# A fused attention and gated feed-forward kernel: a new order for everything up to the middle of block 2

## The chip, the core and the metric

The kernel runs on one core of one Trainium2 chip. The metric is device microseconds of one execution. The kernel before takes 634.76 us (median of three runs, 634.62 to 634.83).

## What is computed

Attention over q, k, v of 4 batches, 8 heads, 768 positions, 64 columns: each query sees the 31 keys around it (|i - j| < 16) and 24 summaries, one for each block of 32 keys (the maximum of the keys, the mean of the values, log 32 added to the score). The result, as 3072 tokens of 512 columns, goes through a gated feed-forward:

```
scores_s = scale * q @ k_sum.T + log(32)         # k_sum: max, v_sum: mean of 32 rows
a = softmax(concat(where(|i-j| < 16, scale * q @ k.T, -1e9), scores_s))
x = a @ concat(v, v_sum)                         # 3072 x 512
h = x @ w_in;  g = h * cos(h);  out = g @ w_out  # 512 -> 2048 -> 512
```

All of it is in float32. For the feed-forward each operand is split into a high part and a rest (the low part), both of a faster float format, and three products (high-high, low-high, high-low) stand for one.

## The kernel before

**Tiling.** The 3072 tokens are 8 blocks of 384, two blocks for each batch. In a block the attention works on four groups a, b, c, d of two heads each (class Group, line 429). The feed-forward works in 128 steps (class Step, line 714): one step is one block and one of 16 slices of 128 hidden columns. Steps s0 to s5 are block 0 with slices 0 to 5, s6 to s21 block 1 with all 16, s22 to s31 block 0 with slices 6 to 15, and from s32 on come blocks 2 to 7.

**The order is written out by hand.** There is no scheduler: ORDER is a list of 2098 tokens, and the last lines of the kernel call one method for each in turn. An engine executes its instructions in the order of the tokens; waits follow from the data, from the buffers and from the eight PSUM banks that the tokens name. Where several engines can do a thing, the token's last letter says which: a is ScalarE, v is VectorE, p is GpSimd.

```
    with tc.manual_schedule(engines=everything):
        prepare()
        for token in ORDER.split():
            who, what, *args = token.split(".")
            one = whose[who]
            getattr(one, does[type(one)][what])(*(int(a) if a.isdigit() else eng_of[a] for a in args))
```

**Tokens of a group**, for instance a0 (group a, block 0):
- q, k, v load (two DMAs each for q and k in the first blocks, three for v, all on the SyncE queue, lines 454, 475, 483); k is loaded once for a batch.
- tk and tq turn k (by halves) and q on TensorE (lines 516, 503); ck and cq place them in SBUF; ks takes the maxima of the keys' blocks on VectorE (line 535).
- ms puts the masks into two PSUM banks by two products (line 554), sc adds the scores (48 products, line 579), mx takes the maxima on VectorE (two reductions, line 597), ex the exponentials with their sums on ScalarE (six, line 614), iv the inverse of the sums on VectorE (lines 624, 627), nm multiplies by it on GpSimd (line 630).
- tp turns the result on TensorE in two parts (line 639), cp places the parts, m copies the means of v beside v (24 rows), va does the values (24 products, line 683), xh and xl make the high and low part of x for the feed-forward (lines 370 or 372, and 376).
- From block 2 on other ways are taken for some of this (kt, qt, kw, z, su, sm, pt, po, pi).

**Tokens of a weight slice**, w0 to w15 (class Slice, line 382): l loads it (two DMAs, lines 391 and 395, 1.02 MB), ab takes one byte of each value apart and sh makes its first bits (ScalarE, lines 403 and 409), fb joins these bits with the rest (VectorE, line 416, two SBUF inputs), hi is the high part (a copy), lo the rest (line 376).

**Tokens of a step**: up is the projection (12 products, line 726), or u one chunk of it, that needs one group of x alone (3 products, line 738); tu, re, si, ga make h * cos(h) on ScalarE (746), VectorE (749), ScalarE (754), VectorE (758); hi and lo are the high and low parts of the result; dh and dl are six and three down products, with sums that stay in three PSUM banks over a run of steps (line 786); ta and st take and store the sums.

**Other tokens.** h0 to h7 are two products each whose result nobody reads (class Warm, line 927). v0_0 and v0_1 are the means of v in batch 0, done by products on TensorE (vm, line 909; ve places them). v1_0 to v1_7 are the means of batch 1: l loads (line 246), s sums (VectorE: lines 261, 270; GpSimd: lines 251, 267, 270). They are wanted by m of block 2.

## Time and profile before

| | |
|---|---|
| median of three runs | 634.76 us |
| the profiled execution, its own time | 633.6 us |
| its span, first to last instruction | 631.9 us |
| chain that ended last | PE 92%, DVE 4%, SPq 2% of the span |
| HBM read and written | 54.43 MB and 16.52 MB |
| first product of the feed-forward | starts at 41.23 us |
| first down product | starts at 58.30 us |

PE is the matmul side of TensorE and PEld its weight load, DVE VectorE, ACT ScalarE, POOL GpSimd, SP SyncE; a name with a q is the engine's queue. A time is in microseconds from the start of the span. A matmul's end is modelled, so that a busy PE need not be at its peak.

### The profile page before, as it was taken

How to read it: one execution, taken by the hardware profiler on the slowest of the kernel's cores; microseconds unless marked ns; L12 is line 12 of the kernel's file. 1: busy time of each engine (PE TensorE's matmuls, PEld its weight loads, DVE VectorE, ACT ScalarE, POOL GpSimd, SP SyncE). 2: the span in 40 equal slices, each digit the busy share in tenths (PEclk: the TensorE clock that was granted, in tenths of full speed). 3: DMA queues.
4: the chain of work that ended last, by engine and by line, in shares of the span. 5: the costliest groups of instructions: out<-in, count | busy, mean ns of one | idle time of the engine just before them, and what ended most of it. 6: DMA issues, size and time to landing. Idle time of an engine off the chain costs nothing.

```text
span 631.9 us, 12130 instructions
## 1 busy us (share of the span) xinstructions
PE 621.1 (98%) x4568; PEld 544.3 (86%) x4568; DVE 422.1 (67%) x814; ACT 323.9 (51%) x606; POOL 204.6 (32%) x218
## 2 busy tenths in 40 slices
...
GB/s 223 261 220 272 297 123 250 145 54 123 122 143 133 112 95 174 102 61 108 109 110 126 117 93 102 121 47 77 108 98 61 117 75 56 114 35 17 1 1 50
DMA packets 170058, 73.52 MB, mean 116 GB/s; under 512 B 136848, under 2 KB 158864, under 8 KB 170000
## 3 DMA queue, kind: packets, MB, share of 16 engines
...
HBM read 54.43 MB, written 16.52 MB: 112 GB/s over the span
## 4 chain that ended last, share of the span: by engine, by line
PE 92%; DVE 4%; SPq 2%; DMA 1%; issue 1%; ACT 1%; POOL 0%; POOLq 0%; DVEq 0%
PE banks L786 41%; PE banks L726 40%; PE banks L683 3%; PE banks L567 3%; PE banks L930 1%; SPq L475 1%; DVE stage L416 1%; PE banks L738 1%; PE banks L579 1%; SPq L483 1%; PE banks L516 0%; PE banks L909 0%; DMA late<-in_v_dram 0%; DMA x<-in_v_dram 0%; DVE kd L535 0%
## 5 line engine op out<-in xcount | busy, mean ns | idle before, releaser
L726 PE MATMUL banks<-xh,w 128*128 128x384 f32 x976 | 255.5, 337 | 0.5 <-DVE t L758 0.5
L786 PE MATMUL banks<-w,gh 128*128 128x512 f32 x768 | 196.5, 392 | 0.1
L726 PEld LDWEIGHTS banks<-xh,w 128*128 128x128 f32 x976 | 176.8, 188 | 3.1 <-issue 0.8
L786 PEld LDWEIGHTS banks<-w,gh 128*128 128x128 f32 x768 | 142.6, 188 | 31.4 <-DVE gh L372 1.8
L726 PE MATMUL banks<-xl,w 128*128 128x384 f32 x488 | 163.2, 334 | 0.0
L376 POOL TENSOR_TENSOR gl<-t,gh 128x384 fp32r<-128x384 f32 x63 | 65.9, 1048 | 283.3 <-DVE gh L372 147.8
L746 ACT ACTIVATE t<-banks 128x384 int32<-128x384 f32 x128 | 62.0, 488 | 126.8 <-PE banks L726 59.7
L749 DVE SCALAR_TENSOR_TENSOR t<-t,banks 128x384 f32<-128x384 int32 x128 | 69.1, 546 | 68.3 <-ACT t L746 67.6
L786 PE MATMUL banks<-w,gl 128*128 128x512 f32 x384 | 108.0, 392 | 0.0
L754 ACT ACTIVATE t<-t 128x384 f32<-128x384 f32 x128 | 65.9, 523 | 63.4 <-DVE t L749 63.1
L726 PEld LDWEIGHTS banks<-xl,w 128*128 128x128 f32 x488 | 91.6, 188 | 0.4
L758 DVE TENSOR_TENSOR t<-t,banks 128x384 f32<-128x384 f32 x128 | 69.4, 547 | 33.1 <-ACT t L754 32.1
L786 PEld LDWEIGHTS banks<-w,gl 128*128 128x128 f32 x384 | 71.6, 188 | 15.7 <-POOL gl L376 0.5
L370 ACT CAST gh<-t 128x384 fp32r<-128x384 f32 x66 | 33.5, 511 | 43.5 <-DVE t L758 25.5
L630 POOL TENSOR_TENSOR sc<-sc,r 128x720 f32<-128x720 f32 x28 | 39.0, 1392 | 43.5 <-DVE r L627 41.0
L602 POOL TENSOR_TENSOR sc<-sc,m 128x720 f32<-128x720 f32 x24 | 34.3, 1433 | 49.6 <-DVE m L594 49.6
L376 DVE TENSOR_TENSOR gl<-t,gh 128x384 fp32r<-128x384 f32 x65 | 36.8, 569 | 12.5 <-ACT gh L370 7.5
L372 DVE CAST gh<-t 128x384 fp32r<-128x384 f32 x62 | 23.1, 373 | 18.1 <-PE banks L786 14.9
L586 DVE SCALAR_TENSOR_TENSOR sc<-banks,mask 128x360 f32<-128x360 f32 x48 | 24.5, 523 | 12.5 <-PE banks L567 12.2
L620 DVE TENSOR_REDUCE r<-sc 128x6 f32<-128x726 f32 x24 | 21.6, 902 | 13.8 <-ACT sc L609 13.8
L376 POOL TENSOR_TENSOR w<-stage,w 128x1024 fp32r<-128x1024 f32 x8 | 19.8, 2470 | 31.3 <-DVE w L372 20.0
L609 ACT ACTIVATE sc<-sc 128x720 f32<-128x720 f32 x24 | 19.4, 807 | 19.0 <-POOL sc L602 18.8
...
## 6 DMA issues: line engine op xcount, KB each, us to landing
...
```

Of the source, the lines that this page charges most:

```text
L370: eng.copy(out=out, in_=in_)
L372: eng.tensor_copy(out=out, in_=in_)
L376: eng.tensor_tensor(out=lo, in0=src, in1=hi.bitcast(F32), op=ALU.subtract)
L586: nc.vector.scalar_tensor_tensor(out=self.sc.rearrange("p (c h) n -> p c h n", h=2)[:, :, hh, :], in0=self.sp[hh], scalar=SCALE, in1=mask[ ...
L602: nc.gpsimd.tensor_tensor(out=self.sc, in0=self.sc, in1=self.m.unsqueeze(2).broadcast_to([P, U, NK]), op=ALU.subtract)
L630: nc.gpsimd.tensor_tensor(out=self.sc, in0=self.sc, in1=self.r.unsqueeze(2).broadcast_to([P, U, NK]), op=ALU.mult)
L726: nc.tensor.matmul(out=self.h, lhsT=w_of(name, self.f)[:, c * P : (c + 1) * P], rhs=x_of(self.blk, part, c), start=n == 0, stop=n == last,)
L746: nc.scalar.activation(out=self.t.bitcast(I32), in_=self.h, func=AF.Copy, scale=1.0 / TWO_PI, bias=0.25)
L749: nc.vector.scalar_tensor_tensor(out=self.t, in0=self.t.bitcast(I32), scalar=-TWO_PI, in1=self.h, op0=ALU.mult, op1=ALU.add)
L754: nc.scalar.activation(out=self.t, in_=self.t, func=AF.Sin, scale=-1.0, bias=-0.5 * math.pi)
L758: nc.vector.tensor_tensor(out=self.t, in0=self.t, in1=self.h, op=ALU.mult)
L786: nc.tensor.matmul(out=accs[self.run][i], lhsT=g[:, i * P : (i + 1) * P], rhs=w_of(name, self.f), start=self.first and n == 0, stop=self.l ...
```

## The change

Only ORDER changes. The last 1539 of its 2098 tokens, from s20.ga (in the middle of block 2's attention), are the same in the same order. The first 559 are the same set of operations in a new order; the PSUM banks and buffers that they name are new in many, and 67 of them name another engine:

| operation | to VectorE | to ScalarE | to GpSimd |
|---|---|---|---|
| low parts (lo) | 7 from GpSimd | | 13 from VectorE |
| high parts (hi) | 10 from ScalarE | 11 from VectorE | |
| placing p, k, q (cp, ck, cq) | 6, 4, 2 from ScalarE | 2, 0, 3 from VectorE | |
| high part of x (xh) | 1 from ScalarE | 3 from VectorE | |
| means (m), windows (kw) | | 2 from GpSimd, 1 from VectorE | |
| sums of v1 (s) | | | 2 from VectorE |

The loads move too: w1 and w0 go ahead of most of q, k and v, and v1_0, which stood after v0_1, goes behind w4. The diff up to s20.ga (the rest only breaks the lines elsewhere):

```diff
--- before.py
+++ after.py
@@ -25,59 +25,59 @@
 ORDER = """
-h0.w.3 h2.w.0 h4.w.1 a0.k a0.q b0.q a0.tk.1.5 c0.k a0.tk.0.0 a0.ms.7.6 a0.ks.1 d0.k b0.tq.3 a0.ks.0 b0.k a0.tq.4 c0.q
-a0.ck.1.a a0.ck.0.a h7.w.5 b0.cq.a a0.cq.v a0.sc c0.tk.0.0 c0.tk.1.2 b0.tk.0.4 c0.ks.0 c0.ck.0.a a0.mx.0 w1.l.6 h5.w.1
-a1.q c0.tq.0 h1.w.1 d0.q a0.ex.0 c0.ck.1.v b0.ck.0.a d0.tk.0.6 c0.ks.1 a0.iv b0.tk.1.1 b0.ks.0 d0.tk.1.2 c0.ms.3.7
-c0.cq.v b0.ms.5.0 c0.sc v0_0.l d0.ck.1.a d0.ks.1 b0.ck.1.a d0.ks.0 b0.ks.1 d0.ck.0.v b0.sc w1.ab.0 b1.q w1.sh c0.mx.1
-h6.w.2 a1.tq.6 a1.ms.1.4 v0_1.l v1_0.l d0.tq.2 a1.cq.v c0.ex.1 d0.cq.a a1.sc d0.ms.6.2 d0.sc b0.mx.2 c1.q w1.fb a0.nm
-w1.hi.v a0.tp.1.3 b0.ex.2 v0_0.vm.0 d0.mx.0 d0.ex.3 v0_1.vm a0.v a0.cp.1.a w1.lo.p c0.iv a1.mx.1 v0_1.ve.a b0.iv
-b1.tq.5 a0.tp.0.3 b1.cq.v b1.ms.2.6 b1.sc w0.l.7 d0.iv c0.nm b0.nm a0.m.p d0.m.p b0.m.p d1.q v1_0.s.0.v a1.ex.0 h3.w.5
-a0.cp.0.v d1.m.p b1.mx.2 c0.m.p c1.tq.3 v1_1.l c0.tp.0.5 d0.nm c0.v a1.iv a1.nm a1.m.p c0.tp.1.0 a0.va.4 c1.ms.7.1 c1.cq.v
-c0.cp.0.v d1.tq.3 d0.v a0.xh.a c1.sc v1_1.s.p w2.l.6 b0.v d1.cq.v a0.xl w0.ab.1 b0.tp.1.3 b0.tp.0.5 c0.cp.1.v w0.sh
-d0.tp.0.4 c0.va.0 b1.ex.1 d0.tp.1.6 v1_2.l c1.mx.0 w5.l.1 w0.fb w0.hi.v a1.v w0.lo.p d0.cp.0.a c1.ex.2 b1.iv d0.cp.1.v
-c1.m.p d1.ms.4.2 c0.xh.v d1.sc c0.xl d0.va.0 b1.nm d1.mx.1 b0.cp.0.a b0.cp.1.v a1.tp.0.7 w2.ab.1 c1.iv a1.tp.1.6 c1.nm
-s1.u.0.3 w2.sh d0.xh.v d1.ex.3 d0.xl b0.va.1 b0.xh.v s0.u.0.5 b0.xl v1_2.s.p s0.u.2 s1.u.2 s1.u.3 a1.cp.0.v c1.tp.1.7
-s1.u.1 s0.u.3 w2.fb w2.hi.v a1.cp.1.a d1.iv d1.v c1.v c1.tp.0.2 s0.u.1 s1.tu.0 w4.l.6 w5.ab.0 a1.va.4 s0.tu.1 w2.lo.v
-w5.sh v1_3.l s0.re d1.nm s1.re s2.u.0.6 s2.u.2 s2.u.3 c1.cp.0.a d1.tp.1.1 c1.cp.1.v c1.va.2 d1.tp.0.0 w3.l.7 s0.si
-w5.fb w5.hi.v d1.cp.1.a b1.tp.0.7 w5.lo.v s1.si s1.ga s0.ga d1.cp.0.a b1.v s2.u.1 d1.va.1 b1.tp.1.0 s5.u.0.5 a1.xh.a
-c1.xh.a w8.l.0 a1.xl s1.hi.0.a s0.hi.1.a d1.xh.v d1.xl s1.lo.0.v s0.lo.1.v w4.ab.1 b1.cp.1.a w4.sh v1_3.s.v s5.u.2
-s2.tu.0 s5.u.3 s2.re b1.m.p v1_4.l s5.u.1 w4.fb s0.dh.1.0.3 s2.si s0.dl s2.ga s2.hi.1.v s2.lo.1.p w3.ab.0 b1.cp.0.v
-c1.xl w4.hi.a s1.dh s1.dl s2.dh s2.dl w4.lo.v b1.va.4 w3.sh s4.u.0.6 s4.u.2 w9.l.1 b1.xh.a w3.fb w3.hi.v b1.xl s4.u.3
-w3.lo.p s4.u.1 w8.ab.1 s5.tu.1 w7.l.7 s6.up.4 v1_4.s.0.v s4.tu.0 s4.re w8.sh v1_5.l s4.si s5.re s3.u.0.2 s5.si w9.ab.0
-w8.fb w10.l.2 s4.ga s4.hi.0.v s11.up.7 s4.lo.0.p s5.ga w9.sh s5.hi.1.a w9.fb s3.u.2 s3.u.3 s3.u.1 w8.hi.a s3.tu.0
-s5.lo.1.v w9.hi.a w6.l.6 s6.tu.1 s10.up.6 w8.lo.p a2.v a2.m s3.re s6.re s5.dh s3.si s3.ga s3.hi.1.v w7.ab.1 w9.lo.v
-s4.dl s3.lo.0.p s4.dh s3.dh v1_5.s.v w7.sh w10.ab.0 s3.dl s5.dl w7.fb w7.hi.v s6.si s6.ga s8.up.2 s6.hi.0.v w10.sh
-s11.tu.0 s6.lo.0.v w10.fb s5.ta.0.a s10.tu.1 w10.hi.a w10.lo.p w7.lo.v s9.up.4 s11.re s10.re s5.ta.1.v s11.si s10.si
-w6.ab.1 s7.up.1 s11.ga v1_6.l s10.ga w12.l.7 v1_6.s.v s10.hi.1.a w6.sh s10.lo.1.v v1_7.l s6.dh.5.7.6 w6.fb w12.ab.0
-s11.hi.0.a s6.dl s11.lo.0.v w6.hi.a s5.ta.2.v s7.tu.1 s8.tu.0 s7.re s10.dh s11.dh s10.dl v1_7.s.v s11.dl w12.sh s7.si
-s8.re w13.l.6 s7.ga s16.up.0 s8.si s8.ga s8.hi.1.a s15.up.1 w12.fb s7.hi.0.a s14.up.2 a2.k s5.st.0 w6.lo.v w12.hi.a
-w13.ab.1 s7.lo.1.p s7.dh a2.kt.1 s15.tu.1 s5.st.1 s15.re w13.sh s5.st.2 s8.lo.0.p w12.lo.v s15.si s15.ga w15.l.7
-a2.kt.0 b2.k s8.dl s8.dh w13.fb w11.l.6 s14.tu.0 s15.hi.0.a s14.re s14.si s7.dl s15.lo.0.v s16.tu.1 s15.dh s15.dl
-s16.re s14.ga s14.hi.1.v s14.lo.1.p s12.up.3 w13.hi.a a2.ks.1 s16.si s16.ga a2.q s16.hi.0.a s16.lo.0.v s12.tu.0
-b2.kt.0 w15.ab.0 s13.up.1 w13.lo.v w15.sh s18.up.0 s19.up.2 b2.kt.1 s13.tu.1 a2.ks.0 c2.k w15.fb b2.ks.0 w11.ab.1
-w11.sh b2.ks.1 s12.re s16.dl s14.dh s12.si s13.re w11.fb s16.dh s12.ga w15.hi.a a2.qt s12.hi.1.a s14.dl w11.hi.v
-s13.si s12.lo.0.v c2.kt.0 s13.ga s18.tu.0 s13.hi.0.a w14.l.6 w11.lo.p s18.re s18.si s18.ga s12.dh s18.hi.1.v s12.dl
-s13.lo.1.v s19.tu.1 c2.kt.1 s18.lo.0.p s19.re d2.k s9.tu.0 s13.dh s9.re w14.ab.1 s19.si w15.lo.p s9.si w14.sh s18.dh
-s18.dl s13.dl s19.ga s9.ga w14.fb s19.hi.0.a w14.hi.a a2.kw.v s9.hi.1.v s17.up.0 s23.up.3 b2.q a2.sc.2.1 w14.lo.p
-b2.kw.a s19.lo.0.v d2.kt.1 d2.kt.0 a2.z.1 s19.dh a2.z.0 s19.dl a2.mx.2 s17.tu.1 s17.re s17.si s9.dh b2.qt s17.ga c2.q
-s9.lo.1.v c2.ks.1 b2.sc.2.4 s17.hi.0.a b2.z.0 c2.ks.0 a2.su a2.ex.0 b2.z.1 s21.up.0 v2_0.l s21.tu.0 b2.mx.0 s17.lo.0.v
-s21.re s21.si b2.su s20.up.4 a2.sm s26.up.1 c2.qt a2.iv s20.tu.1 s20.re c2.kw.a s21.ga c2.sc.0.2 a2.nm s17.dh s17.dl
-s20.si d2.q v2_0.s.1.p a2.pt.0 s20.ga a2.po b2.ex.1 v2_1.l b2.sm c2.z.0 s21.hi.1.a s20.hi.0.a s20.lo.0.v s23.tu.1
...
+h0.w.3 h2.w.0 h4.w.1 a0.k c0.k a0.tk.0.0 a0.q w1.l.6 a0.tk.1.5 c0.q a0.ks.1 a0.ck.0.a w1.ab.0 h7.w.6 a0.tq.6 h5.w.3
+a0.ck.1.v b0.q c0.tk.1.1 h6.w.5 a0.cq.v b0.k a0.ks.0 w0.l.7 d0.k c0.tk.0.2 c0.ck.0.v a0.ms.7.3 c0.ks.1 w1.sh a1.q a0.sc
+h1.w.0 c0.ks.0 a0.mx.1 a0.ex.0 h3.w.2 d0.q v0_0.l b0.tk.1.0 w1.fb c0.ck.1.v b0.ck.1.v b0.tq.7 c0.tq.2 v0_1.l w1.hi.v
+c0.ms.6.4 b1.q b0.tk.0.3 c0.cq.a c1.q a0.v w2.l.6 c0.v b0.ks.1 w0.ab.1 c0.sc a0.iv b0.ck.0.v b0.ks.0 w0.sh b0.ms.2.1
+b0.cq.v a1.tq.3 d0.v c0.mx.2 c0.ex.1 b0.sc b0.v d0.tq.5 a1.ms.6.7 a1.cq.a w0.fb d0.tk.0.0 d0.tk.1.4 a1.sc b0.mx.0
+d0.ck.0.v b0.ex.2 a0.nm d0.ks.0 w1.lo.p a0.tp.0.2 a0.tp.1.1 c0.iv d0.ms.3.0 d0.ks.1 d0.ck.1.a a1.mx.0 w0.hi.a c0.nm
+a0.cp.0.v v0_0.vm.4 d0.cq.v a1.ex.0 v0_1.vm a1.iv v0_1.ve.a a0.cp.1.v w0.lo.p w5.l.1 d0.sc d0.mx.2 c1.tq.6 c0.tp.0.4
+a1.nm d0.m.p a0.m.a b0.iv d1.q b1.tq.2 c1.ms.1.5 b0.nm a0.va.7 d0.ex.3 d1.m.a c1.cq.v c1.sc b1.ms.6.3 b1.cq.v b1.sc
+c0.cp.0.v c0.tp.1.2 d0.iv a0.xh.v a0.xl c1.mx.0 d0.nm w2.ab.1 w2.sh b1.mx.1 c0.m.p s0.u.0.7 d0.tp.1.0 c1.ex.2 b0.m.p
+c0.cp.1.v w2.fb w4.l.6 a1.v c0.va.4 d0.tp.0.2 b1.m.p d0.cp.1.v c1.v c0.xh.a s1.u.0.1 d0.cp.0.v c1.iv b0.tp.0.0 c1.nm
+c0.xl d0.va.5 b0.cp.0.v b0.tp.1.2 b0.cp.1.v s1.u.2 b0.va.4 w2.hi.a a1.tp.0.0 s0.u.2 b1.ex.1 d0.xh.v d0.xl b0.xh.a
+s0.u.3 a1.cp.0.v s1.u.3 w5.ab.0 w2.lo.p s2.u.0.6 c1.m.p b0.xl d1.tq.5 s1.u.1 w5.sh d1.cq.a s0.u.1 d1.ms.0.4 v1_0.l
+s0.tu.1 b1.iv s1.tu.0 w5.fb a1.m.p w3.l.7 s2.u.2 w5.hi.a s1.re b1.nm w5.lo.p a1.tp.1.5 a1.cp.1.v s2.u.3 d1.sc s0.re
+w4.ab.1 d1.mx.0 c1.tp.0.3 s2.u.1 w4.sh a1.va.5 s5.u.0.2 s5.u.2 c1.cp.0.v c1.tp.1.3 w4.fb w4.hi.v s5.u.3 d1.ex.3
+c1.cp.1.a d1.iv s5.u.1 a1.xh.a c1.va.0 w4.lo.v a1.xl b1.tp.0.4 s0.si s4.u.0.3 s1.si s4.u.2 v1_0.s.0.p d1.nm c1.xh.a
+d1.v v1_1.l s0.ga s4.u.3 s0.hi.1.v d1.tp.1.5 s1.ga s4.u.1 d1.cp.1.v w8.l.0 b1.v s0.lo.1.p w9.l.1 w3.ab.0 c1.xl
+s0.dh.7.1.5 d1.tp.0.0 s0.dl s1.hi.0.v s1.lo.0.v w3.sh s1.dh s2.tu.0 s5.tu.1 s2.re d1.cp.0.a s2.si s1.dl w3.fb s2.ga
+v1_1.s.p s2.hi.0.a w3.hi.v d1.va.0 b1.tp.1.6 d1.xh.a s2.lo.1.v w3.lo.p s4.tu.0 s2.dh b1.cp.0.a b1.cp.1.a s5.re s2.dl
+b1.va.4 s5.si s4.re s4.si b1.xh.a s5.ga s3.u.0.6 v1_2.l d1.xl s5.hi.1.a w7.l.7 b1.xl s3.u.2 s3.u.3 v1_2.s.p s3.u.1
+s4.ga w8.ab.1 s4.hi.0.a v1_3.l s8.up.2 w8.sh w9.ab.0 w8.fb w8.hi.a s5.dh s4.lo.0.v s5.lo.1.v w10.l.2 s10.up.0 s3.tu.1
+s4.dl w8.lo.v w9.sh s3.re w9.fb s3.si w6.l.6 s3.ga s4.dh w7.ab.1 w7.sh v1_3.s.v s3.hi.0.a w7.fb v1_4.l w9.hi.a s6.up.3
+s3.lo.0.v s3.dh s6.tu.1 s3.dl s5.dl a2.v v1_4.s.0.p w9.lo.v w7.hi.a s7.up.4 s6.re v1_5.l s5.ta.1.v s10.tu.0 s5.ta.0.a
+s6.si w10.ab.0 s6.ga s5.ta.2.v w7.lo.p s6.hi.0.a a2.q s5.st.2 s10.re s10.si s11.up.3 s5.st.1 s5.st.0 s10.ga w10.sh
+s6.dh.5.7.6 s6.lo.1.p s10.hi.1.a s11.tu.1 s6.dl w6.ab.1 a2.qt v1_5.s.v s11.re v1_6.l s9.up.0 w10.fb s10.dh w10.hi.v
+s11.si s10.lo.1.p w6.sh s11.ga s11.hi.0.v w6.fb s8.tu.0 w12.l.7 s11.dh v1_6.s.v s11.lo.0.p b2.q s10.dl w6.hi.a w10.lo.p
+w6.lo.p s14.up.3 v1_7.l s7.tu.1 s7.re s8.re s7.si s8.si s7.ga s11.dl s7.hi.1.a w13.l.6 s7.dh s15.up.1 w12.ab.0 s8.ga
+v1_7.s.v s8.hi.0.v a2.k w12.sh w13.ab.1 s7.lo.1.v s16.up.4 w12.fb w13.sh w12.hi.a s8.lo.0.p w13.fb a2.kt.0 s16.tu.0
+s15.tu.1 w12.lo.p s8.dl s13.up.2 s15.re s8.dh a2.kt.1 s7.dl s15.si s15.ga s16.re s16.si s15.hi.1.v w15.l.7 s12.up.1
+a2.m s15.lo.0.v s16.ga s15.dh s16.hi.0.v s15.dl w13.hi.a w15.ab.0 s14.tu.1 b2.k w11.l.6 s16.lo.1.v s12.tu.0 s14.re
+s14.si s18.up.4 w15.sh w13.lo.p s14.ga s14.hi.1.v s14.lo.0.p s13.tu.1 w11.ab.1 s12.re s12.si b2.kt.1 a2.ks.0 s16.dl
+w15.fb w11.sh b2.kt.0 s14.dh s13.re s16.dh c2.k s14.dl s19.up.3 s13.si s12.ga b2.ks.0 s12.hi.1.a w11.fb s12.lo.1.v
+s13.ga s18.tu.0 s12.dh w15.hi.v s13.hi.0.a s18.re s12.dl w14.l.6 s18.si w11.hi.a s18.ga s13.lo.0.p s9.tu.1 s13.dh
+c2.kt.1 w11.lo.v a2.ks.1 s18.hi.1.a s18.dh c2.kt.0 s9.re s18.lo.1.p s19.tu.0 s18.dl w14.ab.1 s9.si s26.up.1 s17.up.2
+s9.ga w14.sh w15.lo.p s19.re s9.hi.1.a w14.fb d2.k s19.si c2.ks.1 s13.dl s9.lo.1.p b2.ks.1 w14.hi.v s19.ga a2.kw.a
+w14.lo.v a2.sc.0.3 s21.up.4 b2.qt a2.z.0 s17.tu.1 b2.kw.a s19.hi.0.a s19.dh c2.q a2.z.1 s20.up.3 a2.mx.0 s17.re d2.kt.0
+a2.su d2.kt.1 s19.lo.0.v s17.si s17.ga s21.tu.0 s21.re s17.hi.0.a s19.dl v2_0.l a2.ex.0 c2.ks.0 b2.sc.0.2 b2.z.1 a2.sm
+s21.si s17.lo.0.p s9.dh a2.iv b2.z.0 s17.dh c2.qt s20.tu.1 s23.up.2 s20.re b2.mx.2 c2.kw.a a2.nm d2.q s21.ga a2.pt.1
+b2.su v2_0.s.1.p s17.dl c2.sc.0.4 s20.si s20.ga a2.po b2.ex.1 v2_1.l b2.sm c2.z.0 s21.hi.1.a s20.hi.0.a s20.lo.0.v
...
```

## Rows read from the trace of the kernel before

**Rows 1.** The page: busy us (share of the span) xinstructions of each engine
```profile
PE 621.1 (98%) x4568; PEld 544.3 (86%) x4568; DVE 422.1 (67%) x814; ACT 323.9 (51%) x606; POOL 204.6 (32%) x218
```

**Rows 2.** By stretch: us, PE PEld DVE ACT POOL busy, PEclk, DMA share, GB/s
```profile
0.00:7.00 7.00, 5.56 (x8) 2.36 (x9) 2.80 (x26) 1.28 (x1) 5.39 (x22) 1.00 0.80 166
7.00:31.00 24.00, 23.18 (x393) 16.19 (x393) 17.37 (x41) 17.35 (x73) 12.46 (x21) 1.00 1.09 264
31.00:58.00 27.00, 23.33 (x354) 19.73 (x355) 24.56 (x42) 22.67 (x61) 21.41 (x20) 1.00 0.90 236
58.00:66.00 8.00, 7.94 (x55) 6.13 (x54) 7.75 (x13) 5.38 (x7) 1.02 (x1) 1.00 1.11 307
66.00:145.00 79.00, 79.00 (x463) 71.41 (x463) 67.58 (x114) 61.98 (x90) 28.72 (x18) 1.00 0.65 168
```

**Rows 3.** Timeline and chain: TensorE's steps back to back (start us, us)
```profile
7.99 0.73 PEld L503 LDWEIGHTS banks<-ident,late 128*128 128x128 f32 x6
...
9.78 0.98 PEld L579 LDWEIGHTS banks<-kd,qd 64*64 64x64 f32 x48 [0.76 <-ACT late L509]
...
13.47 1.02 PE L930 MATMUL banks<-ident 128*128 128x512 f32 x2
...
15.75 0.77 PE L554 MATMUL banks<-early 128*128 128x360 bf16 x4
...
23.93 2.78 PE L909 MATMUL banks<-late,early 128*24 128x256 f32 x24
...
70.72 2.08 PE banks L726 x12
...
76.44 6.16 PE banks L786 x27
...
158.20 0.85 PE banks L683 x24
```

**Rows 4.** Timeline and (last) chain: where five steps start on TensorE
```profile
30.91 0.92 PE L683 MATMUL banks<-pt,vn 120*64 120x64 f32 x24
...
41.92 0.92 PE L683 MATMUL banks<-pt,early 120*64 120x64 f32 x24
...
58.30 1.55 PE L786 MATMUL banks<-w,gh 128*128 128x512 f32 x6
...
65.75 0.44 PE L738 MATMUL banks<-xh,w 128*128 128x384 f32 x1
...
130.42 0.78 PE banks L567 x24
```

**Rows 5.** Groups by line and shape: VectorE in 7:31, ScalarE in 31:58
```profile
L597 DVE TENSOR_REDUCE m<-banks 128x3 f32<-128x360 f32 x12 | 5.8, 522 | 0.0
...
L372 DVE COPY pt<-banks 120x512 f32<-120x512 f32 x1 | 0.7, 682 | 0.0
...
L409 ACT ACTIVATE first<-stage 128x1024 int8<-128x1024 f32 x4 | 5.5, 1377 | 0.1
...
L403 ACT ACTIVATE stage<-late 128x1024 f32<-128x1024 int8 x4 | 4.6, 1152 | 1.0 <-POOL w L376 1.0
...
L614 ACT ACTIVATE sc<-banks,m 128x120 f32<-128x120 f32 x6 | 2.1, 372 | 0.0
```

**Rows 6.** Timeline: joins on VectorE, alone and beside GpSimd
```profile
21.86 1.22 DVE L416 SCALAR_TENSOR_TENSOR stage<-late,first 128x1024 int32<-128x1024 int32 x1
...
23.88 2.36 POOL L376 TENSOR_TENSOR w<-stage,w 128x1024 fp32r<-128x1024 f32 x1 [7.23 <-DVE w L372]
...
44.59 1.39 POOL L630 TENSOR_TENSOR late<-late,r 128x720 f32<-128x720 f32 x1
...
44.97 2.09 DVE L416 SCALAR_TENSOR_TENSOR stage<-late,first 128x1024 int32<-128x1024 int32 x1 [0.33 <-POOL sc L630]
```

**Rows 7.** Timeline: a sum of v on GpSimd
```profile
45.94 2.59 POOL L251 TENSOR_TENSOR kn<-kn 96x256 f32<-96x256 f32 x2
...
48.61 1.58 POOL L270 TENSOR_TENSOR vs<-vs,kn 96x64 f32<-96x64 f32 x2
```

189 lines of the change are left out of this document (94 added, 95 removed).

## The prediction

> **What bounds the kernel now.** I read the engine totals first [rows 1]: TensorE is busy for 621.1 of 631.9 us and no other engine for more than 67%. Then the windows [rows 2]: from 66 us on TensorE is busy in all of 79.00 us while VectorE is idle for 11.4 of them, so that an order of work can save nothing there; it can only lose. Before 66 us TensorE has gaps (23.18 of 24 us, 23.33 of 27), and in 31 to 58 us VectorE is busy for 24.56 of 27, GpSimd for 21.41, ScalarE for 22.67: there the other four queues set the time. The granted clock is 1.00 in each window, so I leave it out.
>
> A busy TensorE there still counts warming products and half-fed matmuls, so I measure by **lost time**: the time at which a step starts on TensorE, less the dense price of all that stands before it in the order. The dense prices [rows 3]: a warming product 1.0 us, a transpose 0.12, the two mask products of a group 0.4, its 48 score products 0.98, a values step 0.83 to 0.85, the means 2.8, one projection chunk (3 of 12) 0.52, the six and three down products 1.37 and 0.69 (27 in 6.16). Ahead of the first down product, s0.dh, the order of before has 8 warming products, 16 turned halves, 8 masks, 8 scores, 16 turned exponentials (48 transposes), 7 values, the means and 16 chunks: 8.0 + 5.8 + 3.0 + 7.8 + 6.0 + 5.8 + 2.8 + 8.3 = 47.5 us. It starts at 58.30 [rows 4]: 10.9 lost. By the same count a0's values (30.91, work 25.8) stand at 5.1, b0's (41.92, 34.1) at 7.8, s4's first chunk (65.75, 54.4) at 11.3, and group a2's scores (130.42, 118.7) at 11.7. So 5.1 us go by 31 us, 5.8 in 31 to 58, 0.4 to 66, and 0.4 in the 65 us after.
>
> **The change, part by part.** Work is the same but for engines, and from s20.ga the two orders agree, so the end moves by the difference in lost time. By the prices of the rows the 559 moved steps take 5.9 us less of VectorE and 13 us more of GpSimd (13 low parts and two sums of v move to it, 7 low parts back; two mean copies go on to ScalarE); ScalarE is even, with 11 high parts in and 10 out. I walk the new order queue by queue.
>
> *Loads.* The queue of loads is full (DMA share 1.09 in 7 to 31 us, at 264 GB/s [rows 2]). Weight slices w1 and w0 (1.02 MB each) now stand before a1's q: 4.4 MB (four k of 0.39, four q of 0.2, two slices) land at 7 + (4.4 - 1.2) / 0.264 = 19.3 us, and the second half of the v means, 6.2 MB, at 26. Both are just in time in the walk below, so the loads cost nothing; at 236 GB/s they would cost 1 to 2 us. The loads of v1_0 to v1_7 go behind w4 and w3: that frees 0.4 MB by 40 us.
>
> *To 31 us.* Three warming products (3.0 us) now stand before a0's scores; only one did. They start at 11.9, after 9.78 before [rows 3]. From there a chain: maximum and exp of a0 (an exp is 2.1, a maximum 1.0 [rows 5]) to 15.8; then VectorE places and summarises a0, b0 and c0, takes c0's maximum, and reaches w0.fb at 20.3. That step is held by GpSimd: [rows 6] show it at 1.22 alone and at 2.09 when it begins 0.38 after a GpSimd product of 1.39; it then ended 1.08 after that product. w1.lo.p (2.36) begins at 19.3 here, so w0.fb ends at 22.8. b0's exp (25.5), d0.ck.1 and w0.hi on ScalarE (27.2), a1's exp (29.3) and a0.m (30.9) follow in that queue; a0's values start at 31.45 with 24.5 ahead: 6.9 lost, 1.8 worse than before.
>
> *31 to 45 us.* VectorE has thirteen steps from 29.35 on (two maxima of 1.0, placings of 0.4 to 0.7 [rows 5], the parts of x) before it places c0, at 36.95; w2.fb is held by a copy of means to 38.5; six placings bring b0's values to 41.65, with 32.7 ahead: 9.0 lost against 7.8.
>
> *45 to 66 us.* Here before lost 3.0 more. Of that, sums of v stood in the way: on GpSimd 2.59 + 1.58 [rows 7] for v1_2 alone, while VectorE ran w2 and w5 entirely by itself, both held. Now the low parts of w2 and w5 are GpSimd's and their high parts ScalarE's, and v1_0's sum comes only behind them. ScalarE becomes the pace: from w5.ab at 43.1 to the placing of c1 at 54.0 it does two bytes-apart steps of 1.15, two of 1.38, an exp and the rest of 0.4 to 1.05 [rows 5] with 0.85 of waiting. c1's values start at 54.05 (9.8 lost), s4's chunks at 56.1, behind w4.fb, which v1_0's sum holds for 0.9, and d1's normalising holds s0's high part to 58.3. s0.dh starts at 58.75, but with 48.0 ahead (all of s4 is up already, one values step and 0.75 of transposes are not): **10.8 lost against 10.9**.
>
> *From there.* Before lost 0.4 more by s4's first chunk, in waits for high parts on VectorE. In the new order s1, s2 and d1's values follow with every operand 0.1 to 1 us early, so I charge nothing; then 0.2 for the joints to 130 us, the smaller half of before's 0.4. Sum: 11.0 against 11.7, 0.7 less, of which I keep 0.6 for gaps that a count by hand rounds away. The profiled execution took 633.6 for its span of 631.9; 633.6 - 0.6 = 633.0. It lies 1.2 below the median of the runs, 634.76, so the forecast for the median is **634.1**.
>
> *Bounds of the unknown.* The price that decides is the holding of VectorE. With no holding at all the walk gives 9.2 at s0.dh and 9.4 in the end: 2.3 us faster, 632.5. With each held step at its full price and ScalarE late once (second rival) it is 1.7 us slower. I take full holding, since 2.09 less 1.22 is nearest to it.
>
> [...]
>
> **The rivals.** *The cover is better than I count* (chance 0.30): the holding overlaps waits that the queue has anyway. For it: VectorE is idle for 11.4 us after 66, and it has 5.9 us less to do. Against it: it was busy for 24.56 of 27 us, so there is little for a held step to hide behind. It gives 9.2 to 9.9 lost, 632.5 to 633.1.
>
> *ScalarE takes over as the bound* (0.21), the slower side: from w8.ab to s3's high part ScalarE has four bytes-apart and first-bits pairs, and s3.hi, VectorE's before, now stands behind w7.sh. In the walk it ends at 79.0, and s3.dh's slot on TensorE is 79.1. Each late join pushes it; one such step late costs a bytes-apart and a first-bits step, 1.15 + 1.38 = 2.5 us: 13.3 to 13.5 lost, 1.7 slower, 636.4. It decides once ScalarE reaches w8.ab more than 0.1 us after 68.4. For it: joins held by GpSimd's sums of v. Against: 62.0 of 79 us busy before.
>
> *The order does nothing that counts* (0.07): loads come as late as before, in the same queue, and all is hidden: 634.8.
>
> **How the numbers follow.** My own case has 0.42; its own range is 633.3 to 635.3. A measurement of this kernel can tell 0.2% from no change, 1.27 us. The first rival is faster throughout (0.30), my case in a fifth (0.08): 0.38. ScalarE as the bound is slower by more than that (0.21), with 0.02 from my case: 0.23. The rest, 0.39, is within. The range takes in the first rival's best end and the second's price: 632.0 to 636.4.
>
> **What would show it.** Right: a0's values near 31.5 us, b0's near 41.7, c1's near 54, s0.dh near 58.8 with all of s4 up before it; w0.fb at 2 us or more beside w1's low part on GpSimd; TensorE without a gap after 60. My first steps are wrong if w0.fb takes 1.2 or a0's values come before 30.5. The first rival: s0.dh before 57.5. The second: a gap of 1 to 2.5 us on TensorE between 72 and 85 that a high part on ScalarE ends. Wrong altogether: a gap after 100 us, or one that a transfer ends before 30.

## The result, and the profile after

**The changed kernel is slower: 639.51 us against 634.78 for the kernel before on the same chip, a ratio of 1.0075 (95% interval 1.0046 to 1.0104).** On a second chip it was 639.81 against 633.61, 1.0103 (1.0082 to 1.0124). The forecast was 634.1, range 632.0 to 636.4: outside the range, and on the wrong side. Its executions differ more than those of the kernel before: 638.03 to 642.32 in ten of them, against 633.44 to 634.83 for the kernel before on the same chips.

The profiled execution took 640.97 us, 7.4 more than the profiled one of before. Line numbers of the changed kernel are one less than before's. The page's engine totals, to set beside [rows 1]:

```profile
PE 623.8 (98%) x4568; PEld 546.1 (85%) x4568; DVE 421.7 (66%) x808; ACT 326.2 (51%) x606; POOL 215.1 (34%) x228
```

TensorE's work is the same, yet its busy time is 2.7 us longer. The windows, to set beside [rows 2]:

```profile
0.00:7.00 7.00, 5.56 (x8) 2.36 (x9) 2.80 (x26) 1.28 (x1) 5.40 (x22) 1.00 0.85 171
7.00:31.00 24.00, 20.81 (x329) 14.68 (x327) 17.62 (x36) 16.80 (x59) 11.49 (x18) 0.93 1.05 263
31.00:58.00 27.00, 24.89 (x398) 21.81 (x390) 19.89 (x43) 23.71 (x67) 20.21 (x17) 0.94 0.94 217
58.00:66.00 8.00, 8.00 (x59) 6.56 (x59) 7.37 (x13) 6.01 (x11) 4.80 (x6) 1.00 1.00 264
66.00:145.00 79.00, 75.13 (x424) 66.13 (x424) 65.83 (x100) 55.77 (x84) 31.82 (x23) 1.00 0.63 171
```

Two things were not there before. The granted clock, the column behind the five engines, is below 1.00 in two stretches; and from 66 to 145 us, where TensorE had been busy for all of 79.00 us, it is idle for 3.87. TensorE's waits up to 150 us say where (us in total, times, longest):

```profile
PE banks L502 <- DMA late<-in_q_dram: 3.2, 1, 3.2
PE banks L638 <- issue: 2.1, 1, 2.1
PE banks L785 <- ACT gh L369: 1.5, 1, 1.5
...
PE banks L785 <- DVE gh L371: 1.1, 1, 1.1
PE banks L785 <- DVE gl L375: 1.0, 1, 1.0
```

They stand at a1's turning (17.7 to 20.9 us), before c0's second turned part (36.0 to 38.2), and before the down products of s7 (103.2), s11 (96.6) and s2 (its low ones, 69.0). At none of these steps does TensorE wait in the kernel before. The places of [rows 4] in the timeline, with a0's values, b0's, the first down product and a2's scores:

```profile
32.68 0.92 PE L682 MATMUL banks<-pt,vn 120*64 120x64 f32 x24
...
44.81 0.92 PE L682 MATMUL banks<-pt,early 120*64 120x64 f32 x24
...
60.67 1.55 PE L785 MATMUL banks<-w,gh 128*128 128x512 f32 x6
...
137.04 0.42 PE L566 MATMUL banks<-first,qd 64*64 64x120 f32 x2
```

I go on with the prediction's measure, lost time: the start of a step less the dense price of the TensorE work ahead of it in that kernel's order. The table has it for the kernel before, the changed one (twice profiled), and the experiments, whose numbers are explained below. "66 to 165" is the difference of the columns beside it: what is lost behind s2's first down product, up to a2's values. A trace is that of one execution, which can lie up to 2.6 us from its kernel's median. Ratios are to the kernel before on the same chip, with intervals.

| kernel | a0's values | b0's values | s2's down | a2's values | 66 to 165 | median us | ratio |
|---|---|---|---|---|---|---|---|
| before | 5.1 | 7.8 | 11.1 | 11.7 | 0.6 | 634.78, 633.61 | 1 |
| changed | 8.1 | 12.1 | 12.8 | 19.1 | 6.3 | 639.51 | 1.0075 (1.0046 to 1.0104) |
| 1 changed, again | 7.9 | 9.6 | 10.1 | 16.2 | 6.1 | 639.81 | 1.0103 (1.0082 to 1.0124) |
| 2 q first | 7.8 | 9.5 | 10.2 | 15.9 | 5.7 | 638.27 | 1.0066 (1.0052 to 1.0080) |
| 2 before, load early | 6.8 | 8.7 | 11.9 | 12.4 | 0.5 | 635.03 | 1.0024 (1.0015 to 1.0032) |
| 3 warm | 5.5 | 9.2 | 10.0 | 16.5 | 6.5 | 641.60 | 1.0120 (1.0106 to 1.0134) |
| 4 fill | 8.5 | 8.8 | 9.4 | 15.4 | 6.0 | 639.70 | 1.0088 (1.0075 to 1.0101) |
| 5 v means first | 5.2 | 11.6 | 12.2 | 19.6 | 7.4 | 641.12 | 1.0114 (1.0101 to 1.0127) |
| 6 one letter | 8.9 | 12.6 | 13.2 | 17.9 | 4.7 | 637.84 | 1.0069 (1.0053 to 1.0085) |
| 7 six letters | 9.0 | 10.5 | 11.1 | 16.4 | 5.3 | 638.90 | 1.0082 (1.0066 to 1.0098) |
| 8 late steps | 9.3 | 10.8 | 11.4 | 17.8 | 6.4 | 641.35 | 1.0111 (1.0097 to 1.0125) |
| 9 sums early, q first | 7.5 | 9.6 | 10.6 | 16.9 | 6.3 | 637.16 | 1.0065 (1.0042 to 1.0088) |
| 10 last mend | 7.8 | 10.1 | 10.8 | 15.6 | 4.8 | 639.08 | 1.0091 (1.0070 to 1.0111) |

(Experiments 3 and 4 have 3.06 and 2.04 us more warming products, which count as work and not as lost.) The 7.4 us between the two profiled executions are 1.7 up to s2 (12.8 for 11.1) and 5.7 behind it (6.3 for 0.6). Counted from the start of one step to that of the next, the three waits behind 66 us make up 4.5 of these 5.7: 1.5 at s2, 1.3 at s11, 1.7 at s7.

### The profile page after: what moved, and what is told of

Its sections match the earlier page's. It is cut to its first block, busy times and chain, and to the rows that moved or that the text cites. A ratio compares the mean times of both kernels' runs of the same rounds, so it can differ in the third digit from the quotient of the medians.

```text
span 639.3 us, 12138 instructions
## 1 busy us (share of the span) xinstructions
PE 623.8 (98%) x4568; PEld 546.1 (85%) x4568; DVE 421.7 (66%) x808; ACT 326.2 (51%) x606; POOL 215.1 (34%) x228
## 4 chain that ended last, share of the span: by engine, by line
PE 81%; DVE 7%; ACT 3%; SPq 3%; POOL 3%; DMA 2%; issue 2%; DVEq 0%; POOLq 0%; ACTq 0%
PE banks L785 36%; PE banks L725 36%; PE banks L682 3%; PE banks L566 3%; SPq L453 2%; DVE stage L415 1%; DMA late<-in_q_dram 1%; PE banks L578 1%; DMA late<-in_v_dram 1%; DVE t L757 1%; POOL w L375 1%; DVE gl L375 1%; ACT first L408 1%; ACT gh L369 0%; DVE part_sum L260 0%
## 5 line engine op out<-in xcount | busy, mean ns | idle before, releaser
L375 POOL TENSOR_TENSOR gl<-t,gh 128x384 fp32r<-128x384 f32 x66 | 69.6, 1056 | 272.3 <-DVE gh L371 136.2
L757 DVE TENSOR_TENSOR t<-t,banks 128x384 f32<-128x384 f32 x128 | 69.6, 548 | 35.8 <-ACT t L753 34.6
L375 DVE TENSOR_TENSOR gl<-t,gh 128x384 fp32r<-128x384 f32 x62 | 39.3, 636 | 11.7 <-ACT gh L369 6.4
L375 POOL TENSOR_TENSOR w<-stage,w 128x1024 fp32r<-128x1024 f32 x11 | 26.6, 2424 | 9.1 <-ACT w L369 6.3
L608 ACT ACTIVATE sc<-sc 128x720 f32<-128x720 f32 x24 | 19.3, 806 | 19.4 <-POOL sc L601 19.2
```

The lines of the kernel that those rows point to most:

```text
L375: eng.tensor_tensor(out=lo, in0=src, in1=hi.bitcast(F32), op=ALU.subtract)
L757: nc.vector.tensor_tensor(out=self.t, in0=self.t, in1=self.h, op=ALU.mult)
```

## The experiments

**1. The changed kernel again, as a control.** No edit.

> The changed kernel as it is, once more, beside the kernel before on the same chip, as the measure for the other three. Theory, the losses are the order's own: the gaps before a1's turning (3.2 us), before the 470th matmul (2.1), and at 69, 96.6 and 103 us (1.0, 1.1, 1.5) stand again at the same steps, ratio 1.0046 to 1.0104. Rival, the first two came from one chip's slow transfers: one of them below 1 us.

The waits stood at the same steps: 3.1, 1.1, 1.0, 1.1 and 1.5 us. But this profiled execution took 638.25, 2.7 less, and its windows tell from where:

```profile
31.00:58.00 27.00, 25.91 (x399) 22.57 (x399) 22.71 (x47) 25.68 (x71) 21.52 (x18) 1.00 0.93 228
...
66.00:145.00 79.00, 75.81 (x435) 67.25 (x436) 65.51 (x104) 57.84 (x86) 30.74 (x24) 1.00 0.59 161
```

From 31 to 58 us the clock is 1.00 and the gap before c0's second part 1.1 us instead of 2.1; s2's down product then has 10.1 lost, one less than in the kernel before. The stretch from 66 us on loses the same 6 us in both. So, by these two executions, the changed kernel has a **steady loss behind 66 us** and a **changing one around 36 us**.

**2. The first gap: q of a1 and d0 loaded ahead of w0.** Besides, w0's first bits and join go behind c0's exponential and b0's maximum.

```diff
-a0.ks.0 w0.l.7
+a0.ks.0 a1.q d0.q w0.l.7
-w1.sh a1.q a0.sc
+w1.sh a0.sc
-h3.w.2 d0.q v0_0.l
+h3.w.2 v0_0.l
-b0.ks.0 w0.sh b0.ms.2.1
+b0.ks.0 b0.ms.2.1
-c0.ex.1 b0.sc
+c0.ex.1 w0.sh b0.sc
-a1.ms.6.7 a1.cq.a w0.fb d0.tk.0.0
+a1.ms.6.7 a1.cq.v d0.tk.0.0
-d0.ck.0.v b0.ex.2
+d0.ck.0.v w0.fb b0.ex.2
```

> The changed kernel with q of a1 and d0 loaded ahead of weight slice w0, a1 placed by VectorE, and w0's first bits and join behind c0's exponential and b0's maximum; all else as changed. Theory: the changed kernel loses 4.8 us between 17.7 and 26 us because a1's q lands late (3.2 us of waiting on TensorE) and because the granted clock is 0.50 for some 3.5 us after that gap (about 1.5 us more). Then the gap before a1's turning shrinks below 1.5 us, the granted clock stays at 1.00 from 20 to 25 us, a0's values start at 31.5 or earlier (32.7 in the changed kernel), and the time falls by 2 to 4 us from 639.5, to 635.5 to 637.5. Rival, the other queues would have held TensorE just as long: a0's values stay at 32.5 to 32.9 and the time falls by less than 1 us.

The wait for a1's q went, and the clock stayed at 1.00, but a0's values started at 32.33, against 32.39 in the control: the rival's sign. TensorE waited elsewhere, 1.5 us for c0's exponential (ScalarE), and 1.5 us in four smaller waits up to 27.1 us. The windows 20 to 25 and 36 to 41 us, and a step of ScalarE ahead of c0's exponential:

```profile
20.00:25.00 5.00, 2.66 (x59) 1.83 (x57) 2.38 (x5) 5.00 (x21) 1.20 (x1) 1.00 1.09 313
...
36.00:41.00 5.00, 3.99 (x60) 3.51 (x61) 4.68 (x10) 5.00 (x18) 2.52 (x4) 1.00 0.87 256
```

```profile
19.61 1.14 ACT L402 ACTIVATE stage<-late 128x1024 f32<-128x1024 int8 x1 [3.08 <-DMA late<-in_moe_w_out_dram]
```

ScalarE, the fourth column, is busy for all of 20 to 25, and its queue holds TensorE as long as the wait for q had. But a load stands behind this too: w0, which now comes after the two q, landed later, and ScalarE was idle for 3.08 us before it could take w0's bytes apart, a step that stands ahead of c0's exponential. So this edit exchanges one late load for another, and it does not show that the loads cost nothing; in experiment 5, which moves w0 and its steps back, a0's values come 2.6 us earlier.

The median is 1.2 and 1.5 us below the changed kernel's two, between the theory's 2 to 4 and the rival's less than 1, with executions of 637.1 to 638.6 instead of 638.0 to 642.3. Where this comes from is not shown: the profiled execution is only 0.3 below the control's, and from 36 us on the clock is 1.00 in both.

The load alone, put into the kernel before (w0's load from behind b1's scores to ahead of a1's q):

```diff
-h5.w.1 a1.q
+h5.w.1 w0.l.7 a1.q
-b1.sc w0.l.7 d0.iv
+b1.sc d0.iv
```

> The kernel before with one part of the change alone: the load of weight slice w0 (1.02 MB) ahead of a1's q. Theory, the loads decide the first 30 us: a1's q lands near 20.4, the second half of v's means near 28.6 (24.6 before), a0's values start 2 to 3.5 us later than 30.91, and the time rises by 1.5 to 3 us. Rival, the slack of the other queues hides it: a0's values within 1 us of 30.91 and the time within 0.5 us.

635.03 against 633.61, ratio 1.0024 (1.0015 to 1.0032): 1.4 us, a little under the theory's 1.5 to 3. In that order the late load does cost: a0's values start at 32.52, 1.6 later than before. In the timeline a1's turning now waits:

```profile
20.75 0.52 PE L504 MATMUL banks<-ident,late 128*128 128x128 f32 x3 [0.77 <-DMA late<-in_q_dram]
```

**3. The clock: six more warming products in the first gap.**

```diff
-b0.cq.v a1.tq.3
+b0.cq.v h3.w.5 h4.w.5 h7.w.5 a1.tq.3
```

> The changed kernel with six more warming products (three tokens, 1.02 us each) ahead of a1's turning, so that TensorE is busy while it waits for a1's q; the wait itself stays. Theory, the fall of the granted clock comes from the idle 3.2 us: the clock stays at 1.00 from 21 to 25 us, b0's scores take 1.1 us instead of 1.86, a0's values start 1.3 to 1.6 us earlier, and the time falls by about 1.5 us, to 638.0. Rival, the clock falls at this place whatever TensorE did before, or the lost 1.5 us is given back to a wait behind it: b0's scores stay at 1.9, or the time falls by less than 0.5 us.

One-microsecond windows of the changed kernel, TensorE alone (busy, clock, DMA share, GB/s), beside the first and second gap:

```profile
20.00:21.00 1.00, 0.14 (x1) 0.96 0.99 288
21.00:22.00 1.00, 1.00 (x12) 0.50 0.68 160
...
23.00:24.00 1.00, 1.00 (x19) 0.50 1.07 343
...
25.00:26.00 1.00, 1.00 (x41) 1.00 1.37 275
...
37.00:38.00 1.00, 0.00 (x0) 1.00 1.04 309
38.00:39.00 1.00, 0.85 (x4) 0.50 1.02 269
...
40.00:41.00 1.00, 1.00 (x19) 0.50 0.89 270
```

Behind each of these two gaps the granted clock is 0.50 for some 3.5 us, and 1.00 again after that. With the warming products the clock was 1.00 throughout 20 to 25 us and b0's scores took 1.09 instead of 1.86:

```profile
21.13 1.09 PE L578 MATMUL banks<-kd,late 64*64 64x96 f32 x48
...
29.09 0.40 PE L908 MATMUL banks<-late,early 128*24 128x256 f32 x2 [1.48 <-DMA late<-in_v_dram]
...
37.75 0.46 PE L578 MATMUL banks<-kd,late 64*64 64x24 f32 x6 [1.37 <-issue]
```

So at this place the lower clock came behind 3.2 us of idle time and stayed away when products filled them, as the theory said. The time did not fall but rose by some 2 us, with 3.06 us of products added: what was won at 22 us was given back at 29 to the means of v, whose load is late too (the second line). The idle time is not all there is to it: gaps of 1.1 us (control) and 1.9 us (experiment 10, second version) were followed by 1.00, this one of 1.37 by 0.57 from 38 to 42 us.

**4. The second gap: the supply of instructions.** The wait before c0's second part is put down to "issue": nothing that the profile shows. But in the kernels that have it, it stands ahead of the same matmul by count, the 470th (experiment 5, second version: the 471st), and the last line of the fence above shows it at b1's scores once six products have been put in ahead. So it goes with the place in the program. The DMA view of the changed kernel, stretch 34.6 to 35.6 us (queue and kind, packets, MB, share of 16 engines), shows what comes just before it:

```profile
q8 instruction: 1, 0.02, 9.1%
```

From 26.5 to 34.6 us this queue moved none. In the whole span it has 36 packets, 0.59 MB: 16 KB each, and by my estimate one for every 254 instructions, if they are the 4568 matmuls and as many weight loads. In all sixteen profiled executions that have the gap, the step behind it started 2.6 to 3.1 us after the packet did (3.1 and 2.9 in the two of the changed kernel, 2.8 in the second version of experiment 5). That TensorE waits there for its instructions is inferred from this and from the edit below; the profile itself names no cause. Four warming products inside the dense run of small products ahead of it:

```diff
-c1.sc b1.ms.6.3
+c1.sc h4.w.0 h7.w.0 b1.ms.6.3
```

> The changed kernel with four more warming products (two tokens, 1.02 us each) ahead of b1's masks, that is inside the dense run of small products before the gap at 36.0 to 38.2 us. In all five kernels of this order so far that gap stands before the same matmul by count (the 470th), also where six added products moved another step to that place. Theory, TensorE waits for its instructions, which 120 small products in 3.4 us use up faster than they come: then the two us are spent inside the wait, the gap before c0's second turned part falls below 0.5 us, this part still starts at 38.0 to 38.5, the granted clock stays at 1.00 from 36 to 42 us, and the time falls by 0.5 to 1.5 us (less where the clock was 1.00 anyway). Rival, the gap belongs to that step or to the clock time and not to the count: c0's second part starts 2 us later, at 40, and the time rises by 2 us.

```profile
34.87 1.98 PE L929 MATMUL banks<-ident 128*128 128x512 f32 x4
...
37.09 1.09 PE L578 MATMUL banks<-kd,late 64*64 64x96 f32 x48
38.10 0.43 PE L638 MATMUL banks<-ident,late 128*120 128x128 f32 x2
```

The gap is gone, c0's part starts at 38.10 (38.15 in the changed kernel), and the clock is 1.00 from 36 to 42: the theory in the trace. The profiled time is 1.6 below the changed kernel's first profile and 1.2 above the control's, and the ratio is no better; its executions lie within 0.6 us of each other. That the added work costs what the gap had cost, where the clock would have stayed up anyway, would fit, but is not shown.

**5. Everything early.** The v means loaded ahead of w0 too, w0's four steps later, and a0's turned parts ahead of the means; behind 66 us both versions have the edit of experiment 8, with w13's load moved ahead. A first version had a0's turning behind a1's exponentials, which overwrote a0's; its values are thus of other numbers, its work the same.

```diff
-a0.ks.0 w0.l.7 d0.k c0.tk.0.2
+a0.ks.0 a1.q d0.k d0.q c0.tk.0.2
-v0_1.l w1.hi.v c0.ms.6.4 b1.q
+v0_1.l w0.l.7 w1.hi.v c0.ms.6.4 c1.q b1.q
-b0.ex.2 a0.nm d0.ks.0 w1.lo.p a0.tp.0.2 a0.tp.1.1
+b0.ex.2 a0.nm d0.ks.0 w1.lo.p d0.cq.v a0.tp.0.6 d0.ck.1.v d0.ks.1 a0.tp.1.5
...
```

The first version's expectation, and the second's:

> The late steps' edit, and in the first 36 us the loads nearly as in the kernel before: q of a1 and d0 and the v means ahead of w0, with w0's four steps moved behind a1's exponential, the means placed by VectorE and GpSimd, and a1's and d0's banks exchanged. Theory, up to 31 us the changed kernel is late by its loads (v's means land at 26.2 us, 24.6 before): the means' products start at 24 instead of 27.4, a0's values at 29.5 to 31 (30.9 before, 32.7 changed), ratio 0.995 to 0.999. Rival, ScalarE and VectorE bind this stretch whatever the loads do: a0's values at 32 or later and a ratio of 0.999 to 1.003.

> The same late edit, and the first 36 us with q of a1 and d0 and the v means loaded ahead of w0, a0's probabilities turned ahead of the means in banks of their own, and w0's four steps and means on engines with room. Theory: the gap before a1's turning goes (below 0.5 us), a0's values start at 29 to 30.5 (30.91 in the kernel before), the gap of the instruction supply stays below 1 us or is covered, and the ratio to the kernel before is 0.995 to 0.999. Rival, VectorE binds from 30 to 40 us whatever comes earlier: c0's values at 37.5 or later, ratio 0.999 to 1.003.

The first took 639.49 us, 1.0088 (1.0075 to 1.0101), and had no gap before c0's second part; a0's values came at 29.65, but TensorE waited 1.5 us for VectorE ahead of b1's scores, and by b0's values 9.9 us were lost. In the second a0's values came at 29.76, earlier than in the kernel before, and b1's scores 2.9 us earlier than in the changed kernel. TensorE reached the place of the gap sooner and stood there for longer:

```profile
36.41 0.37 PE L638 MATMUL banks<-ident,late 128*120 128x128 f32 x1 [3.04 <-issue]
```

From 36 to 42 us the clock was then 0.50:

```profile
36.00:38.00 2.00, 1.59 (x6) 0.50 0.77 168
38.00:42.00 4.00, 4.00 (x35) 0.50 1.01 306
```

By b0's values all was lost again, 11.6. In the sixteen executions with this gap the step behind it starts between 36.4 and 38.7 us, whatever comes before it. So a0's values came as the theory had it, and the ratio did not.

**6 and 7. Behind 66 us: GpSimd's low parts.** One letter, w3's low part on VectorE:

```diff
-s2.lo.1.v w3.lo.p s4.tu.0
+s2.lo.1.v w3.lo.v s4.tu.0
```

> The changed kernel with one letter changed: w3's low part on VectorE instead of GpSimd. Theory, s2's low part (2.78 us on VectorE beside it, 0.55 alone) is held by that GpSimd instruction alone: it takes 0.55 to 0.7 us, the gap of 1.0 us before s2's low down products goes, and 1 us is gained at 70 us, all of it given back by 100 us only if the later waits grow. Rival, it waits for its operands or a buffer: it still ends at 2 us or more after its start, and the gap stays.

The changed kernel, then the one letter:

```profile
66.15 2.38 POOL L375 TENSOR_TENSOR w<-stage,w 128x1024 fp32r<-128x1024 f32 x1 [2.82 <-DVE w L371]
66.17 2.78 DVE L375 TENSOR_TENSOR gl<-t,gh 128x384 fp32r<-128x384 f32 x1
```

```profile
66.62 0.56 DVE L375 TENSOR_TENSOR gl<-t,gh 128x384 fp32r<-128x384 f32 x1
```

s2's low part takes 0.56 us for 2.78, the wait before its low down products is gone, and the loss behind 66 us falls from 6.1 to 4.7: the theory. The other two waits stay at 1.1 and 1.5. w3's low part was GpSimd's in the kernel before too; there s2's low part was as well, and the change put it on VectorE beside w3's. The same on six low parts (w3, w7, w10, w6, w12, w13; the kernel before had four of them on VectorE, not five):

```diff
-s2.lo.1.v w3.lo.p s4.tu.0
+s2.lo.1.v w3.lo.v s4.tu.0
-w6.hi.a w10.lo.p w6.lo.p s14.up.3
+w6.hi.a w10.lo.v w6.lo.v s14.up.3
...
```

> The changed kernel with six letters changed and nothing moved: the low parts of w3, w7, w10, w6, w12 and w13 on VectorE, where the kernel before had five of them. VectorE gets 7.3 us more work between 66 and 120 us, where it is idle for 13. Theory, the holding costs more than the work: s2's low part takes 0.55 to 0.7 us, the second sum of v1_6 0.45 instead of 2.27, s16's low part 0.55 instead of 2.57, the wait at 69 us goes and the one at 103 us shrinks below 1 us; 1.5 to 2.5 us faster than the changed kernel, ratio 1.004 to 1.008. Rival, the added work stands ahead of the gates and delays them as much: the waits at 96.6 and 103 us stay or grow, and the ratio is 1.009 or more.

The last addition of v1_6's sum in the changed kernel, and s16's low part:

```profile
98.70 2.27 DVE L269 TENSOR_TENSOR vs<-vs,part_sum 96x64 f32<-96x64 f32 x1
...
114.86 2.58 DVE L375 TENSOR_TENSOR gl<-t,gh 128x384 fp32r<-128x384 f32 x1
```

and with the six letters:

```profile
96.52 0.22 DVE L269 TENSOR_TENSOR vs<-vs,part_sum 96x64 f32<-96x64 f32 x1
...
113.67 0.56 DVE L375 TENSOR_TENSOR gl<-t,gh 128x384 fp32r<-128x384 f32 x1
```

An addition of 64 columns that takes 0.22 us was held to 2.27, ten times its price. In the changed kernel GpSimd runs low parts of weight slices beside both of these steps, from 98.50 to 103.22 us and from 114.44 to 117.02; with the six letters VectorE has them. Not every VectorE step is longer there: beside another such low part, from 109.97 to 112.59 us, a residue took 0.52 us and a gate 0.56.

How much holding there was in all can be told from VectorE's total. The six parts are 7.3 us of work, and yet it is busy for 421.9 us, against 421.7 in the changed kernel (422.4 in the control); the page of the six letters:

```profile
PE 623.8 (98%) x4568; PEld 546.7 (86%) x4568; DVE 421.9 (66%) x814; ACT 325.8 (51%) x606; POOL 202.3 (32%) x222
```

So, by this count, some 7 us of what VectorE did in the changed kernel was holding, and with it gone the loss behind 66 us fell by 0.8 only (6.1 to 5.3). s11's wait grew from 1.1 to 1.9, and the clock fell to 0.50 behind it. The work added ahead of s11's gate is not the reason, since VectorE stood idle in front of it, in the changed kernel as here:

```profile
91.16 0.58 DVE L520 STREAM_TRANSPOSE qd<-qn 128x384 f32<-128x384 f32 x1 [1.98 <-DMA qn<-in_q_dram]
```

```profile
89.22 0.58 DVE L520 STREAM_TRANSPOSE qd<-qn 128x384 f32<-128x384 f32 x1 [1.82 <-DMA qn<-in_q_dram]
```

It waits for a2's q, whose load stands behind a sum's load in the queue; v1_5's sum, s11's residue, w10's join and high part and s11's gate come behind this step. Nor was s7's high part earlier: two low parts (2.35 us) now stand where the held addition stood, s7's down product follows s11's by 6.9 us instead of 6.7, and its wait shrank to 0.2 because TensorE ran at a granted clock of 0.50 from 94.7 to 98.1 us. The outcome lies between the two that were expected: a smaller wait at 103 us, a larger one at 96.6.

**8. All three late waits at once.** w3's and s11's low parts to VectorE, w10's high part behind s11's, s7's turns earlier, the sums v1_6 and v1_7 later:

```diff
-s11.hi.0.v w6.fb
+s11.hi.0.v s11.lo.0.v w10.hi.v w6.fb
-s11.dh v1_6.s.v s11.lo.0.p b2.q
+s11.dh b2.q
-s7.ga s11.dl
+s7.ga v1_6.s.v v1_7.l s11.dl
-w12.fb w13.sh
+w12.fb v1_7.s.v w13.sh
...
```

> The changed kernel, the order up to 60 us left as it is; w3's and s11's low parts on VectorE instead of GpSimd, w10's high part behind s11's, s7's turns ahead of w6's high part, the sum v1_6 (with the load behind it) behind s7's gate and v1_7's sum behind the join of w12, so that no step of another order stands behind its transfer. Theory: the three waits at 69.0, 96.6 and 103.2 us are made by VectorE steps that are held beside low parts on GpSimd or stand behind sums: all three end below 0.5 us and the time falls by 2.5 to 3.6 us, to a ratio of 1.002 to 1.0035 to the kernel before. Rival, the three operands are late because everything before 60 us is late, and the waits only shift: the ratio stays above 1.005.

The three waits ended at 0, 0.4 and 0 us; s7's went with the sum v1_6 behind s7's gate. The time did not fall, for a new one stood at s12's projection:

```profile
PE banks L725 <- DVE t L757: 2.5, 1, 2.5
PE banks L785 <- ACT gh L369: 0.9, 1, 0.9
PE banks L785 <- DVE gh L371: 0.4, 1, 0.4
```

The load of w13, now behind a later sum on the load queue, landed as late as in the changed kernel (its bytes are taken apart from 105.35 us on, 106.07 there) although TensorE was five microseconds ahead, and s15's turns stand behind w13's bytes on ScalarE. Together with experiment 2's edit:

> q of a1 and d0 ahead of w0 (the edit of the first experiment) together with the late steps' edit. Theory, the two losses add, and with both gone the first down product starts at 58.1 (58.30 in the kernel before, with 0.5 us more work done by then) and nothing is lost behind it: ratio 0.998 to 1.000 to the kernel before. Rival, the late steps are late again at other places: ratio above 1.003.

It was the same, 1.0103 (1.0079 to 1.0127). Then the late steps' edit by itself, with w13's load moved ahead:

> The late steps' edit as before, and w13's load ahead of v1_6's sum and v1_7's load, since there it landed as late as in the changed kernel and stopped s12's projection for 2.5 us by way of s15's turns, which stand behind w13's bytes on ScalarE. Theory: the gaps of 2.5 and 0.9 us at 109 and 128 us go too, nothing above 0.5 us is left between 60 and 150 us, and the time is 3 to 5 us below the changed kernel beside it. Rival, with TensorE this early the next transfer or step is late: another gap of 1.5 us or more behind 100 us, and less than 2 us gained.

1.0109 (1.0086 to 1.0133), and the same wait was 2.6 us: now a2's k, behind v1_7's sum, was late, and s15's residue stands behind a2's k on VectorE. An earlier attempt, with two sums moved behind w6's join and s8's gate, had done worse:

> The changed kernel with w3's low part on VectorE instead of GpSimd, and two sums of v with the loads behind them later (v1_5 behind the join of w6, v1_6 behind s8's gate). Theory: three waits on VectorE and ScalarE at 69.0, 96.6 and 103.2 us (1.0, 1.1 and 1.5 us, 3.6 in all) come from steps that are held beside GpSimd's low parts or stand behind sums of v; all three go and the time falls by 3 to 3.6 us, to 636.0 to 636.5. Rival, the gaps only move to the next late operand: less than 1.5 us, with a gap of 1 us or more on TensorE elsewhere between 66 and 110 us. Both leave the stretch up to 60 us as it is.

s8's high part stood behind a sum that waited for its transfer, TensorE waited 5.2 us for it, and the ratio was 1.0206 (1.0181 to 1.0231); with experiment 2's edit 1.0170 (1.0156 to 1.0183):

> Both edits at once, q of a1 and d0 ahead of w0 and the later sums of v. Theory, the two losses lie in different stretches and add: 5 to 7.5 us less than the changed kernel, 632 to 634.5, no slower than the kernel before. Rival, what the first edit gains by 31 us is lost again before 60 us in the queues that I counted as the bound: no better than the later sums alone by more than 1 us, 635 to 636.5.

**9. The chain of the sums shortened.** v1_3 to v1_7 share one buffer and a2's k comes behind the last, so each load waits for the sum before it:

```diff
-w6.l.6 s3.ga
+w6.l.6 v1_3.s.p v1_4.l s3.ga
-w6.ab.1 a2.qt
+w6.ab.1 v1_5.s.v v1_6.l a2.qt
-s10.lo.1.p w6.sh
+s10.lo.1.p v1_6.s.p w6.sh
...
```

> The changed kernel, the order up to 60 us left as it is; w3's and s11's low parts on VectorE, w10's high part behind s11's, and the chain of v's sums for batch 1 shortened, since v1_3 to v1_7 share one buffer and a2's k waits behind the last: v1_3 and v1_6 on GpSimd where it is idle, v1_5 ahead of a2's q, each load right behind the sum before it, and a2's two squares of k behind s15's gate. Theory: the late order of these sums is what stops TensorE from 66 to 115 us; with the chain early and off VectorE nothing above 0.5 us is left between 60 and 130 us, and the time is 3.5 to 4.5 us below the changed kernel (639.8 beside the kernel before at 633.6): ratio 1.002 to 1.005, with the first 60 us still late. Rival, in this order some transfer or operand is always late there: a gap above 1 us, ratio above 1.007.

> The same, and q of a1 and d0 loaded ahead of w0 as in the first experiment. Theory, both losses go: ratio 0.998 to 1.002, the granted clock at 1.00 from 20 to 46 us in most executions. Rival, the gap of the instruction supply before the 470th matmul with the clock behind it stays in some executions and decides: ratio 1.003 to 1.006.

Without the early edit 640.71 us, ratio 1.0089 (1.0068 to 1.0111); with it 637.16, 1.0065. The first is its rival's outcome, the second lies just above its rival's range: no wait above 1.3 us was left behind 66 us in the first, none above 0.8 in the second, but there were seven and nine of them, and 6.8 and 6.3 us of lost time. Two of them followed from s16's low part, still held to 2.56 us beside w13's. The second's profiled execution took 639.72 us; four of its six took 636.5 to 637.3, so that they lose less than this trace shows, and where is not known.

**10. All known causes.** Experiment 9 with the early edit, six low parts on VectorE and three steps reordered; then once more with s8's parts ahead of v1_7's sum:

```diff
-w10.lo.v v1_7.s.v
+w10.lo.v s8.hi.0.v s8.lo.0.v s7.lo.1.v w6.lo.v v1_7.s.v
-w12.hi.a s8.lo.0.p w13.fb
+w12.hi.a w13.fb
...
```

> q of a1 and d0 ahead of w0, the shortened chain of v's sums, and all low parts of weight slices between 66 and 120 us (w3, w7, w10, w6, w12, w13) on VectorE as in the kernel before, w10's and w6's behind s8's gate; s7's and s15's residues ahead of the joins they stood behind, w13's load ahead of v1_7's. Theory: what is left in that stretch after each mend comes from one cause, a VectorE step held beside a GpSimd low part (s16's low part still took 2.56 us instead of 0.55, and s14 and s18 were late by 0.8 each behind it); without those parts less than 1.5 us is lost from 64 to 150 us (6.2 in the run before), and the ratio is 0.997 to 1.002. Rival, the order has TensorE too close behind the gates, whatever holds them: more than 3 us are lost there again, ratio above 1.004.

> The run before the last (all known causes mended) once more, with s8's high and low part and s7's low part ahead of v1_7's sum on VectorE and s8's low part on VectorE: there the sum waited for its transfer until 101.6 us, s8's high part stood behind it, its low part on GpSimd took 3.46 us, and TensorE waited 3.8 us for it. Theory, this was the last of the late steps: less than 1.5 us is lost from 64 to 150 us (1.1 was lost up to that place, 0.1 behind it), 3 to 4 us less than that run, ratio 1.002 to 1.005, what remains being the first 46 us (gap of the instruction supply, and the clock in some executions). Rival, another gate is late as soon as this one is not: a further gap above 1.5 us behind 100 us, ratio 1.007 or more.

The first (639.98 us, 1.0102, 1.0084 to 1.0119) had 1.1 us lost from 64 to 98 us, and then one wait of 3.8, with its cause in two lines of the timeline, VectorE and GpSimd:

```profile
101.58 1.06 DVE L260 TENSOR_REDUCE part_sum<-kn 96x64 f32<-96x512 f32 x1 [2.79 <-DMA kn<-in_v_dram]
```

```profile
103.60 3.46 POOL L375 TENSOR_TENSOR gl<-t,gh 128x384 fp32r<-128x384 f32 x1 [9.13 <-DVE gh L371]
```

The second took that away, and TensorE's waits from 60 to 150 us were:

```profile
PE banks L785 <- ACT gh L369: 1.0, 1, 1.0
PE banks L725 <- DVE t L757: 0.8, 1, 0.8
PE banks L566 <- DVE t L757: 0.2, 1, 0.2
```

Its profiled execution, 637.53, is its fastest, and 4.8 us are still lost behind s2. Neither outcome is the one expected: no wait above 1.5 us, as the theory had it, and a ratio of 1.0091, as the rival had it. No version beat the kernel before.

## Why the prediction was wrong

**Up to s2 the walk was about right, in part by luck.** w0's join began at 19.75 and ended at 22.18, 1.08 us after w1's low part on GpSimd, as I had worked out; a0's values were to come at 31.45 and came at 32.4 to 32.7; the first down product, forecast at 58.75 with 10.8 lost, came at 58.08 with 10.1 in the control (60.67 and 12.7 in the first profile). The gain from 41 to 66 us was real: where the kernel before loses 3.3 us from b0's values to s2's down product, the changed one loses 0.7 and 0.5. But I had expected 1.8 to go there, and nothing for a1's q, the clock and the instructions; that these errors cancel in the control is luck.

**The step that failed** is the last of the walk: "In the new order s1, s2 and d1's values follow with every operand 0.1 to 1 us early, so I charge nothing; then 0.2 for the joints to 130 us". It lost 6.1 to 6.3 there, where the kernel before loses 0.6, and three operands that came late make up most of it:
- s2's low part (1.5 us) was held beside w3's on GpSimd, 2.78 us for 0.56. One letter gives 1.4 back, so this is shown.
- s7's high part (1.7 us) stood behind the sum v1_6, whose addition was held, 2.27 us for 0.22. With the sum behind s7's gate (experiment 8) the wait is gone, so it is shown that the sum made it, but not how much of it the holding is.
- s11's high part (1.3 us) stood behind a step for which VectorE had waited 1.98 us, until a2's q landed. In experiment 9, with v1_5's sum and the loads behind it earlier, this idle time is 0.38 us and s11's wait is gone; as w10's high part had been moved too, the cause is shown only in part.

Holding, which I had counted up to 60 us and then stopped counting, is thus not the whole of it: experiment 7 took some 7 us of it away and gained 0.8. What remains, some 1.2 us, was not traced.

Why none of the mends of experiments 6 to 10 gave back more than 1.4 us also stays open: they took one releaser after another away, and mostly another took its place. A shorter way from a step's projection to its down products does not explain it as a whole. By the dense prices, the TensorE work between the two is 15.1 us before and 15.3 after in the mean of s2 to s19, 12.4 in both for s7, and longer in the new order for s2 (7.3 and 12.5); s11's is much shorter (19.5 and 5.5), and so is s6's (18.7 and 6.9).

**Terms that were mis-sized or missing.** "The granted clock is 1.00 in each window, so I leave it out": true of before, but behind two new gaps it was 0.50 for some 3.5 us. The gap of the instruction supply had no term. The two together are the 2.7 us between the two profiled executions of the changed kernel. "5.9 us less of VectorE": its busy time fell by 0.4 (422.1 to 421.7), and the other 5.5 are holding by my estimate. "The loads cost nothing": a1's q landed at 20.7 us instead of 19.3 and TensorE waited 3.2 for it. The rate was not too high, since 278 GB/s came from 7 to 20.7 us; but by then 5.0 MB had come, for the 4.4 that I had counted, and d0's q and half of the means' rows had been issued behind a1's q by then. By experiment 2 this wait alone can go without a gain, as w0 is late instead; by experiment 5 a0's values can come 2.6 us earlier with w0 out of the way.

**The rivals.** Better cover: near it up to s2 in the control (10.1, where I gave 9.2 to 9.9; the first down product at 58.08, not before 57.5), not behind it. ScalarE as the bound from 72 to 85 us: no gap there at all; it was on the right side with the wrong place. "Wrong altogether: a gap after 100 us, or one that a transfer ends before 30": both came.
